# Weight loads ordered behind SyncE's rows, r.(u k) of two units on TensorE, and new tables for a planned RWKV-6 and FFN kernel

## The chip, the cores and the metric

The kernel runs on one core of one Trainium2 chip. The metric is the device time in microseconds (us) of an execution; for the kernel before it is 173.24 us, the median of 3 runs (173.14, 173.24, 174.6).

## What is computed

The reference has two stages. The first is a linear attention with a decaying state (RWKV-6), for 4 batches, 8 heads, 768 steps and head size 48:

```
for t in range(S):
    cur = u * k_t (outer) v_t
    y_t = r_t @ (state + cur)
    state = w_t[:, None] * state + k_t (outer) v_t
```

The second is a feed-forward network on the 3072 rows of y (384 wide; d_ff is 1024):

```
h = ((y @ w1) * (y @ w2)) @ w3
out = h @ w_out
```

All inputs are float32 in HBM, and the output is float32 of 3072 x 384.

## The kernel before, in words

**Units and chunks.** The 768 steps are cut into 6 chunks of 128. A unit is one chunk of one or two batches: units 0 and 1 are chunk 0 of batches 0 and 1, unit 2 is chunk 0 of batches 2 and 3, and units 3 to 12 are the two halves of the chunks 1 to 5. For each unit the function `unit` makes: `ln` (ScalarE: logarithm of w, line 638), `cs` and `ct` (TensorE: prefix sums of it with the triangular matrix LT, lines 647 and 654), `ne` and `e` (ScalarE: exponentials, 661 and 667), `Kt` (VectorE: k times the inverse decay, 672), transposes of r and Kt (`trr`, `trk`, 736 and 755) with their evictions `RT` and `KT` (741, 760), the product `m` of the two (774), its causal mask (`msk`: VectorE with the mask, line 780, or a copy on ScalarE, 783, with a select `maff` on GpSimd, 786), and `y` (809 for the state's part, 818 for the chunk's own). The state goes on by `kv` (864), `T` (871) and `S` (875).

**r.(u k).** The term with u is a number for each row and head, the sum over the head of r k u. The kernel makes it with `rk` (the product r k, line 677), `ruk` (times u_bc, which is u on all 128 partitions, 712) and `dg` (VectorE's sum over 48 elements, 716). `dv` multiplies v by it (718), and `yb` (830) adds dv to y. For the units in the set `PE_DIAG`, which is empty, the code has another way: transpose `rk` on TensorE (`rkt`), evict it (`rke`), multiply it by `u_blk`, a 384 x 8 block form of u (`d`), and copy the result out (`dcp`).

**Blocks.** y is transposed (`yt`, 847; `xT`, 852) and goes into 8 blocks of 128, 128, 256 and then 512 rows: units 0, 1, 2, then two units each. For each block the function `block` makes groups of `a` and `b` (x times w1 and w2, line 907), copies a out (`asb`, 916, two buffers), multiplies (`abT`, 920), and makes the output tiles `o` (929), `osb` (937) and their stores (942). Instead of two products, w3 and w_out are multiplied once: for each of 8 slices of w3, `wt` transposes it (596), `w3Te` evicts, `wm` multiplies it with w_out (608) and `w34e` evicts (613). No `o` can start before all 8 slices of w34 are there. The group a or b number z of a block needs one half of w1 or w2 (`w1_0`, `w1_1`, `w2_0`, `w2_1`).

**Loads.** The rows of w, k, r and v are loaded per unit for chunk 0 (`win_0` to `vin_2`), and by whole chunks afterwards (`win_3` is chunk 1, `win_5` chunk 2, and so on). Only `win_0` and `win_1` are issued by SyncE (`SP_LOADS`); all others, w1 and w2 in two halves, w3 in four quarters (`w3_0` to `w3_3`, each for two slices), w_out (`wo`) and u go out on GpSimd's queue, between GpSimd's own arithmetic. The rows of chunk 3 lie in the memory of w3 and wait for all `wt`.

**Order.** The order of all work is not written by hand. Each step is an `op` with an engine, an assumed duration, what it reads and writes, and a priority: its place in the program plus `RANK` of its kind plus `STEP` of its name; the smaller goes first. `Program.schedule` (from line 241) plays the steps in assumed time: on each engine that is free it takes the ready step of least priority whose PSUM banks can be had. GpSimd issues no load while the assumed end of its queue lies over `AHEAD` = 6000 ns ahead. `late` adds a dependency to the planner that the data don't have. The order found is then emitted; on the chip each engine works through its own list in order and waits for data. For loads the base of the priority is -10000 plus the place in `LOADS`. `ENGINE` says for the steps that can run on two engines which one takes them.

Of the kernel before, what the change touches and what calls it, by code (L numbers as in the profile page):

```python
# [16 lines left out]
    "KT": -38550, "Kt": -111832, "RT": 5515, "S": -11396, "Sb": 6495, "Sc": -932, "T": -60474, "a": -27703,  # L17
    "abT": -127179, "asb": -32208, "b": -15810, "cs": -59092, "ct": -970, "dg": 88898, "dtk": 10929, "dtr": -20063,
    "dty": -16475, "dv": -5126, "e": -21254, "gate": -14530, "kv": -15949, "ln": 72613, "m": -36962, "maff": -125562,
    "mask": 13249, "msk": -38101, "ne": -7835, "o": 62061, "ones": 17890, "osb": -54919, "pads": -19246, "rk": 73060,  # L20
    "rpad": 11555, "rpads": 6817, "ruk": 32687, "state": -53300, "store": 4513, "table": 12635, "trk": -56488,
    "trr": -71123, "ub": -15816, "ubc": 5038, "w34e": -43757, "w3Te": -48083, "wm": 54280, "wt": -87740,
    "xT": -131752, "y": -73194, "yb": -115233, "ys": 35037, "yt": -99587,
# [3 lines left out]
    "table": 70008.5, "ones": 60179, "LT": -1.5, "I128": 4.5, "pads": 98002, "rpads": 71930, "state0": 136111,  # L27
    "mask": 73935.5, "u": -1, "ub": 82542, "ubc": 76980.5, "w1_0": -1, "w1_1": -5, "wo": -2, "w3_0": -22, "w3_1": -3,
    "gate": 32463, "wt_0": 154172.5, "w3Te_0": 129818, "wm_0": 15188, "w34e_0": 129029, "wt_1": 154703,
    "w3Te_1": 130597.5, "wm_1": 15215.5, "w34e_1": 147138, "wt_2": 157233, "w3Te_2": 152054, "wm_2": 14976.5,  # L30
    "w34e_2": 148425.5, "wt_3": 157108, "w3Te_3": 153375, "wm_3": 15191, "w34e_3": 146990.5, "wt_4": 157683.5,
    "w3Te_4": 133999, "wm_4": 15136, "w34e_4": 145249, "wt_5": 157815.5, "w3Te_5": 149717, "wm_5": 15123.5,
    "w34e_5": 148851, "wt_6": 158569, "w3Te_6": 133971.5, "wm_6": 16223.5, "w34e_6": 144357.5, "wt_7": 158300,
    "w3Te_7": 149762, "wm_7": 14896, "w34e_7": 144603, "rpad3": 93022.5, "win_0": 21, "kin_0": 1, "rin_0": -0.5,
    "vin_0": -1, "ln_0": 2548, "cs_0": 125775.5, "ct_0": 66598, "ne_0": 83308.5, "e_0": 103240.5, "Kt_0": 194792.5,
    "rk_0": 10112.5, "ruk_0": 50257, "dg_0": -1654, "dv_0": 81249.5, "trr_0": 137833.5, "RT_0": 77645,
    "trk_0": 123546.5, "KT_0": 120493.5, "m_0_0": 103205.5, "msk_0_0": 121058, "maff_0_0": 201058.5, "y_0": 139438,
    "yb_0": 202437, "yt_0": 164599.5, "xT_0": 214714, "kv_0": 82166, "T_0": 143490.5, "S_0": 86842, "Sc_0": 83411.5,
    "a_0_0": 92637, "b_0_0": 83851, "asb_0_0": 114728.5, "abT_0_0": 214609, "a_0_1": 94836, "b_0_1": 80692,
    "asb_0_1": 115024.5, "abT_0_1": 209346, "o_0_0": 10003.5, "osb_0_0": 157512, "store_0_0": 4916, "win_1": 17,  # L40
    "vin_1": 5, "ln_1": 3415.5, "cs_1": 126255, "ct_1": 67602, "ne_1": 83529, "e_1": 104051, "Kt_1": 194830.5,
    "rk_1": 14562.5, "ruk_1": 47917, "dg_1": -5616, "dv_1": 92256.5, "trr_1": 137223.5, "RT_1": 81684,
    "trk_1": 124248, "KT_1": 120444, "m_1_0": 105234, "msk_1_0": 120873, "maff_1_0": 201454, "y_1": 141265.5,
    "yb_1": 203525, "yt_1": 164161, "xT_1": 214216.5, "kv_1": 84030.5, "T_1": 148735.5, "S_1": 86860.5,
    "Sc_1": 83039, "a_1_0": 97109, "b_1_0": 83800.5, "asb_1_0": 113342.5, "abT_1_0": 215398.5, "a_1_1": 91588,
    "b_1_1": 85615, "asb_1_1": 113497, "abT_1_1": 201257, "o_1_0": 9463, "osb_1_0": 159063.5, "store_1_0": 1566.5,
    "win_2": -4, "kin_2": -1, "rin_2": -7, "vin_2": 3, "ln_2": 10032, "cs_2": 125219.5, "ct_2": 68023.5,
    "ne_2": 90468.5, "e_2": 103110, "Kt_2": 192412.5, "rk_2": 3076, "ruk_2": 55529, "dg_2": -8338.5, "dv_2": 92032.5,
    "trr_2": 138240.5, "RT_2": 82374.5, "trk_2": 122481.5, "KT_2": 121357, "m_2_0": 102992, "msk_2_0": 124482,
    "maff_2_0": 212398, "m_2_1": 101072.5, "msk_2_1": 121512.5, "maff_2_1": 200856, "y_2": 143006.5, "yb_2": 197826,  # L50
    "yt_2": 168808.5, "xT_2": 219125.5, "kv_2": 83980, "T_2": 147552, "S_2": 98226.5, "Sc_2": 81915.5,
    "a_2_0": 97125.5, "b_2_0": 85352.5, "asb_2_0": 114484.5, "abT_2_0": 209778, "a_2_1": 91099, "b_2_1": 79819,
    "asb_2_1": 114887.5, "abT_2_1": 209146.5, "a_2_2": 97517, "b_2_2": 85273, "asb_2_2": 113263, "abT_2_2": 232260,
    "a_2_3": 97213.5, "b_2_3": 84677, "asb_2_3": 113260.5, "abT_2_3": 201082.5, "o_2_0": 8844.5, "osb_2_0": 158890.5,
    "store_2_0": 1560.5, "o_2_1": 9477.5, "osb_2_1": 156818.5, "store_2_1": 1516, "win_3": -6, "kin_3": -1,
    "rin_3": -1, "vin_3": 3, "ln_3": 10067, "cs_3": 123222, "ct_3": 70704.5, "ne_3": 90160, "e_3": 103517,
    "Kt_3": 199901.5, "rk_3": 8960.5, "ruk_3": 45468, "dg_3": -15223, "dv_3": 79040.5, "trr_3": 140863,
    "RT_3": 68568.5, "trk_3": 126558.5, "KT_3": 112504.5, "m_3_0": 106283, "msk_3_0": 141483, "maff_3_0": 211595.5,
    "m_3_1": 106688, "msk_3_1": 143460.5, "maff_3_1": 203735, "ys_3": 34763.5, "y_3": 142623, "yb_3": 200956,
    "yt_3": 168610.5, "xT_3": 217450.5, "kv_3": 85570, "T_3": 146670.5, "S_3": 89980, "Sc_3": 86574, "ln_4": 9654.5,  # L60
    "cs_4": 128220.5, "ct_4": 70214.5, "ne_4": 89951.5, "e_4": 103121.5, "Kt_4": 199813.5, "rk_4": 5913.5,
    "ruk_4": 49888, "dg_4": -15188, "dv_4": 110729.5, "trr_4": 140354, "RT_4": 68490, "trk_4": 125796,
    "KT_4": 143661.5, "m_4_0": 106275, "msk_4_0": 142101.5, "maff_4_0": 211692.5, "m_4_1": 106372.5,
    "msk_4_1": 141939.5, "maff_4_1": 211792, "ys_4": 34948.5, "y_4": 143017.5, "yb_4": 200903.5, "yt_4": 169292,
    "xT_4": 216637, "kv_4": 85986.5, "T_4": 134260, "S_4": 94111, "Sc_4": 102131.5, "a_3_0": 97359.5,
    "b_3_0": 86039.5, "asb_3_0": 133262, "abT_3_0": 231821.5, "a_3_1": 98771.5, "b_3_1": 86942, "asb_3_1": 136083,
    "abT_3_1": 229014.5, "a_3_2": 99107, "b_3_2": 86889, "asb_3_2": 134171.5, "abT_3_2": 229364, "a_3_3": 98952,
    "b_3_3": 87455, "asb_3_3": 134988.5, "abT_3_3": 229202.5, "o_3_0": 9791, "osb_3_0": 157499.5,
    "store_3_0": 4960.5, "o_3_1": 9352.5, "osb_3_1": 157275, "store_3_1": 4700, "o_3_2": 9888.5, "osb_3_2": 156319.5,
    "store_3_2": 4817, "o_3_3": 11928, "osb_3_3": 157320.5, "store_3_3": 5242.5, "win_5": 91976.5, "kin_5": 95199,  # L70
    "rin_5": 87329.5, "vin_5": 96011.5, "ln_5": 31462, "cs_5": 129257.5, "ct_5": 72093, "ne_5": 111671,
    "e_5": 124931.5, "Kt_5": 216926, "rk_5": 32516, "ruk_5": 56279.5, "dg_5": 14395, "dv_5": 109999, "trr_5": 142134,
    "RT_5": 96247, "trk_5": 127883, "KT_5": 140462.5, "m_5_0": 108808.5, "msk_5_0": 141236.5, "maff_5_0": 225164,
    "m_5_1": 108320, "msk_5_1": 140542.5, "maff_5_1": 224679.5, "ys_5": 38812, "y_5": 144993.5, "yb_5": 219879.5,
    "yt_5": 170492.5, "xT_5": 234218, "kv_5": 87022, "T_5": 162591, "S_5": 99705.5, "Sc_5": 103063.5, "ln_6": 29771,
    "cs_6": 129221.5, "ct_6": 71742.5, "ne_6": 111649.5, "e_6": 124630, "Kt_6": 216456, "rk_6": 15353.5,
    "ruk_6": 72232, "dg_6": 16055.5, "dv_6": 94137.5, "trr_6": 142019, "RT_6": 99915, "trk_6": 127371.5,
    "KT_6": 142440, "m_6_0": 108259.5, "msk_6_0": 140086.5, "maff_6_0": 225008, "m_6_1": 107960, "msk_6_1": 140043,
    "maff_6_1": 223327, "ys_6": 36889.5, "y_6": 144567.5, "yb_6": 219458, "yt_6": 171191.5, "xT_6": 235962.5,
    "kv_6": 86830.5, "T_6": 162909.5, "S_6": 99533, "Sc_6": 103343.5, "a_4_0": 98375.5, "b_4_0": 89760.5,  # L80
# [79 lines left out]
DMA_KR = set(range(9, 13))  # L160
DMA_Y = set(range(9, 13))
DMA_R = set(range(9, 13))
PE_DIAG = set()

BLOCKS = [[0], [1], [2], [3, 4], [5, 6], [7, 8], [9, 10], [11, 12]]

# [189 lines left out]
def kernel(  # L356
# [13 lines left out]
    nc = tc.nc  # L370
# [601 lines left out]
    with tc.manual_schedule():  # L972
        for o in order:
            o.fn(o.eng) if o.alt else o.fn()
# [30 lines left out]
```

## Time and profile before

| | |
|---|---|
| median of the runs | 173.24 us |
| the profiled execution | 174.64 us |
| its span, first to last instruction | 172.9 us |
| TensorE busy | 154.2 us (89%), 1696 matmuls |
| VectorE busy | 123.1 us (71%) |
| ScalarE busy | 99.2 us (57%) |
| GpSimd busy | 106.7 us (62%) |
| mean granted TensorE clock | 0.98 |
| GpSimd's DMA queue | 79024 packets, 15.86 MB |

In the profile PE is TensorE's matmul, PEld its weight load, DVE VectorE, ACT ScalarE, POOL GpSimd and SP SyncE; "POOL L549 kin" is the issue of a load, not its transfer. Times count from the start of the span. In the rows by stage the numbers are: stage, its length, then busy us (and instructions) of PE, PEld, DVE, ACT and POOL, the granted TensorE clock, the DMA share and GB/s. In a timeline a row is start, duration, engine, line, operation, output and inputs, shapes and count. The chain of waits is the work that ended last, followed back from the end: start, duration, what.

### The profile page before, as it was taken

The numbers are of one execution on the slowest core, as the hardware profiler recorded it, in microseconds if no ns is written. First come the engines' busy times: TensorE is split into PE (matmuls) and PEld (weight loads), VectorE is DVE, ScalarE is ACT, GpSimd is POOL, SyncE is SP. The second block draws the span as 40 slices with busy tenths as digits, with TensorE's granted clock in tenths as the row PEclk, the third lists the DMA queues.
The fourth block names the chain that finished last, engine by engine and source line by source line (L and its number), as shares of the span: only waits on it lengthen the run. The fifth ranks groups of instructions, "written<-read, shape, count | busy, mean of one in ns | idle before, by whom it ended". The sixth has DMA issues, their size and how long they took to land.

```text
span 172.9 us, 4084 instructions
## 1 busy us (share of the span) xinstructions
PE 154.2 (89%) x1696; PEld 98.8 (57%) x1708; DVE 123.1 (71%) x155; ACT 99.2 (57%) x134; POOL 106.7 (62%) x90
## 2 busy tenths in 40 slices
PE   0466489999989999999999999999999999999991
PEld 0254368998667666646675555645556455455560
DVE  5076995979897289999777997896689574544310
ACT  4437776674616977569669656957457524232331
POOL 7999985769796999599879969724413600000000
PEclk9999957999999999999999999999999999999999
DMA  6999999999999999999999998698135802111132
GB/s 93 154 190 189 227 179 169 160 207 172 203 182 178 102 144 127 211 185 216 171 186 249 133 89 46 127 187 198 38 64 101 238 20 48 25 49 45 45 122 107
DMA packets 96363, 24.12 MB, mean 139 GB/s; under 512 B 88632, under 2 KB 94264, under 8 KB 96344
## 3 DMA queue, kind: packets, MB, share of 16 engines
q0 software_dynamic: 79024, 15.86, 110.6%
q1 hardware_dynamic: 17320, 8.00, 18.9%
q8 instruction: 13, 0.21, 0.5%
q14 instruction: 6, 0.05, 0.1%
HBM read 27.79 MB, written 4.72 MB: 188 GB/s over the span
## 4 chain that ended last, share of the span: by engine, by line
PE 60%; DMA 12%; DVE 11%; POOL 10%; issue 4%; ACT 1%; DVEq 0%; POOLq 0%; ACTq 0%
PE banks L907 29%; PE banks L929 11%; PE banks L608 6%; DMA w_bf<-in_v_dram 6%; DMA kin<-in_k_dram 4%; PE banks L818 2%; POOL rin L549 2%; DVE Mbf L780 2%; POOL Mbf L786 2%; DVE abT L920 2%; DMA KRT<-Kt 2%; PE banks L774 2%; PE banks L596 2%; PE banks L654 2%; PE banks L864 2%
## 5 line engine op out<-in xcount | busy, mean ns | idle before, releaser
L907 PE MATMUL banks<-xT,w_bf 128*128 128x512 bf16 (+2 forms) x372 | 68.1, 330 | 1.0 <-DVE abT L920 0.2
L907 PEld LDWEIGHTS <-w_bf 128*128 128x128 bf16 x384 | 33.9, 101 | 26.4 <-issue 1.3
L920 DVE TENSOR_TENSOR abT<-a_sb,banks 128x1024 bf16<-128x1024 f32 (+1 forms) x28 | 29.8, 1067 | 21.0 <-PE banks L907 18.9
L916 ACT COPY a_sb<-banks 128x1024 f32<-128x1024 f32 (+1 forms) x28 | 24.8, 891 | 25.1 <-PE banks L907 21.4
L929 PE MATMUL banks<-w,abT 128*128 128x384 bf16 x192 | 34.0, 326 | 0.0
L929 PEld LDWEIGHTS <-abT 128*128 128x128 bf16 x192 | 18.3, 98 | 11.8
L786 POOL TENSOR_SCALAR_AFFINE_SELECT Mbf<-Mbf 128x1024 bf16<-128x1024 bf16 x14 | 15.3, 1099 | 7.8 <-ACT Mbf L783 7.8
L937 ACT COPY osb<-banks 128x384 f32<-128x384 f32 x20 | 9.6, 480 | 16.4 <-PE banks L929 16.4
L783 ACT CAST Mbf<-banks 128x1024 bf16<-128x1024 f32 x14 | 13.9, 1018 | 2.1 <-PE banks L774 2.0
L718 POOL TENSOR_TENSOR dv<-vin,dg 128x768 bf16<-128x768 bf16 (+1 forms) x7 | 10.0, 1431 | 6.6 <-DMA xT<-dv 3.4
L667 ACT ACTIVATE eT<-banks 128x1024 f32<-128x1024 f32 (+1 forms) x13 | 12.4, 956 | 2.4 <-PE banks L654 2.4
L654 PE MATMUL banks<-LT,lw 128*128 128x128 bf16 x96 | 8.0, 227 | 6.4 <-ACT lw L638 6.4
L780 DVE TENSOR_TENSOR Mbf<-banks,mask 128x1024 bf16<-128x1024 f32 x10 | 12.0, 1218 | 1.3 <-PE banks L774 1.3
L661 ACT ACTIVATE banks<-banks 128x768 f32<-128x768 f32 (+1 forms) x13 | 9.7, 749 | 4.9 <-PE banks L647 4.8
L830 DVE TENSOR_TENSOR dv<-banks,dv 128x768 bf16<-128x768 f32 (+1 forms) x13 | 11.6, 890 | 1.2 <-PE banks L818 1.1
L716 DVE TENSOR_REDUCE dg<-rk 128x16 f32<-128x768 bf16 (+1 forms) x13 | 11.5, 887 | 0.3
L638 ACT ACTIVATE lw<-win 128x768 bf16<-128x768 f32 (+1 forms) x11 | 8.3, 787 | 5.6 <-DMA win<-in_w_dram 5.6
L608 PE MATMUL banks<-wo_bf,w3T 128*128 128x384 bf16 x64 | 11.2, 326 | 0.0
L677 POOL TENSOR_TENSOR rk<-rin,kin 128x768 bf16<-128x768 bf16 x6 | 9.9, 1649 | 1.8 <-DMA rin<-in_r_dram 1.8
L601 ACT COPY w3T<-banks 128x1024 bf16<-128x1024 bf16 x7 | 6.9, 1014 | 7.1 <-PE banks L596 7.1
L654 PEld LDWEIGHTS <-lw 128*128 128x128 bf16 x96 | 6.3, 102 | 7.8 <-ACT lw L638 6.9
L672 DVE TENSOR_TENSOR Kt<-kin,banks 128x768 bf16<-128x768 bf16 (+1 forms) x11 | 9.5, 875 | 1.5 <-DMA kin<-in_k_dram 1.4
(83 smaller groups left out, 241.5 us busy)
## 6 DMA issues: line engine op xcount, KB each, us to landing
out_dram<-osb SPq DMA_DIRECT2D x24, 192.0 KB, 2.1
win<-in_w_dram POOLq DMA_DIRECT2D x4, 768.0 KB, 9.6
w_bf<-in_moe_w_dram POOLq DMA_DIRECT2D x4, 512.0 KB, 9.6
w_bf<-in_moe_w_dram POOLq DMA_DIRECT2D x4, 384.0 KB, 9.1
kin<-in_k_dram POOLq DMA_DIRECT2D x4, 384.0 KB, 7.7
rin<-in_r_dram POOLq DMA_DIRECT2D x4, 384.0 KB, 8.5
vin<-in_v_dram POOLq DMA_DIRECT2D x4, 384.0 KB, 8.7
wo_bf<-in_moe_w_out_dram POOLq DMA_DIRECT2D x1, 768.0 KB, 10.5
```

The source lines that it names most:

```text
L608: nc.tensor.matmul(o[:, :DM], lhsT=w3T[fi % 2][:, gi, :], rhs=wo_bf[:, gi, :], start=(gi == 0), stop=(gi == FI - 1))
L654: nc.tensor.matmul(o[:, b, q, :], lhsT=LW[:, b * H + 2 * q:b * H + 2 * q + 2, :].rearrange("t h d -> t (h d)"), rhs=LT, start=True, stop=True)
L667: nc.scalar.activation(ET[:, :, 1:], o[:, :nb * HP, :], Act.Exp)
L716: op("DVE", dve(N), lambda: nc.vector.reduce_sum(dgs, rks, axis=AX.X), r=[f"rk{s}"], w=[f"dg{s}"], prio=pr + 9, name=f"dg_{t}")
L780: nc.vector.tensor_mul(Mbf[m].rearrange("s j q t -> s (j q t)"), o.rearrange("s j f -> s (j f)"), mask.rearrange("s q t -> s (q t)"))
L783: nc.scalar.copy(Mbf[m].rearrange("s j q t -> s j (q t)"), banks[:, g.at(MM):g.at(MM) + 2, :])
L786: nc.gpsimd.affine_select(Mbf[m].rearrange("s j q t -> s (j q) t"), Mbf[m].rearrange("s j q t -> s (j q) t"), compare_op=Alu.is_gt, fill=0 ...
L830: nc.vector.tensor_add(ybs.rearrange("t b (q e d) -> t e (b q) d", e=2, d=D), o, dvs.rearrange("t (b q e) d -> t e (b q) d", b=nb, e=2))
L907: nc.tensor.matmul(o[:, q * T // TB, q % (TB // T), :], lhsT=wt[:, di, fi * P:(fi + 1) * P], rhs=xT[x][:, di, :T], start=(di == 0), stop=( ...
L916: nc.scalar.copy(a_sb[sa][:, :nbk * TB], banks[:, g.at(A):g.at(A) + nbk, :].rearrange("p k t -> p (k t)"))
L920: nc.vector.tensor_mul(abT[x][:, f[0]:f[0] + G, :T].rearrange("p i t -> p (i t)"), a_sb[sa][:, :nbk * TB], banks[:, g.at(Bk):g.at(Bk) + nb ...
L929: nc.tensor.matmul(banks[:, g.at(O), :DM], lhsT=abT[x][:, fi, tt * P:(tt + 1) * P], rhs=w34[:, fi, :], start=(fi == 0), stop=(fi == FI - 1))
```

## The change

Four things are done together. First, `wload` (w1, w2, w_out, w3) and the loads of w on GpSimd's queue get `late=SP_ROWS`: in the planner they become ready only when SyncE's two loads of w have ended. Second, `PE_DIAG` becomes {1, 2}: units 1 and 2 form r.(u k) by TensorE. Third, `RANK`, `STEP` and `ENGINE` are replaced throughout. Fourth, code for filler matmuls in TensorE's idle places comes in (`idle`, `fill`, a tile `warm`), with `WARM` and `FILL` both 0.0.

```diff
 STEP = {
-    "mask": 73935.5, "u": -1, "ub": 82542, "ubc": 76980.5, "w1_0": -1, "w1_1": -5, "wo": -2, "w3_0": -22, "w3_1": -3,
...
+    "mask": 57278, "u": 6, "ub": 71274, "ubc": 93101, "ublk": 75393.5, "ublk2": 108242.5, "w1_0": -2, "w2_0": 2,
+    "w1_1": -12.5, "w2_1": -2, "wo": -1, "w3_0": -4, "w3_1": -2, "w3_2": -1, "w3_3": -1, "gate": 22348.5,
...
+    "abT_1_1": 217906.5, "o_1_0": -4539, "osb_1_0": 161989, "store_1_0": 1175.5, "win_2": -3, "kin_2": 2,
+    "rin_2": -11, "vin_2": 3, "ln_2": -13119, "cs_2": 124194, "ct_2": 65213, "ne_2": 81535.5, "e_2": 111671,
...
 ENGINE = {
-    "ruk_0": "DVE", "dv_0": "POOL", "KT_0": "ACT", "msk_0_0": "DVE", "xT_0": "ACT", "S_0": "POOL", "osb_0_0": "ACT",
-    "rk_1": "DVE", "ruk_1": "DVE", "dv_1": "DVE", "KT_1": "ACT", "msk_1_0": "ACT", "xT_1": "ACT", "S_1": "DVE",
-    "osb_1_0": "ACT", "rk_2": "POOL", "ruk_2": "DVE", "dv_2": "POOL", "KT_2": "ACT", "msk_2_0": "DVE",
...
+    "ruk_0": "DVE", "dv_0": "DVE", "KT_0": "ACT", "msk_0_0": "ACT", "xT_0": "ACT", "S_0": "DVE", "osb_0_0": "ACT",
+    "rk_1": "DVE", "rke_1": "ACT", "dcp_1": "ACT", "dv_1": "DVE", "KT_1": "DVE", "msk_1_0": "ACT", "xT_1": "DVE",
+    "S_1": "POOL", "osb_1_0": "ACT", "rk_2": "DVE", "rke_2": "DVE", "dcp_2": "ACT", "dv_2": "DVE", "KT_2": "ACT",
...
-PE_DIAG = set()
+PE_DIAG = {1, 2}
+
+WARM, FILL = 0.0, 0.0
...
+    SP_ROWS = [f"SP{x}_{t}" for x, t in sorted(SP_LOADS)]
...
         op(eng, 60 if eng == "SP" else 650 + 270 * nb, lambda: e.dma_start(dst[:, b0 * H:(b0 + nb) * H, :D], ap),
-           r=FREED if c % NI == NI - 1 else (), w=[f"{src}in{c % NI}_{b}" for b in range(b0, b0 + nb)] + ["rows_" + src] * (c == NC - 1), prio=turn_of(f"{src}in_{t}"),
+           late=SP_ROWS if src == "w" and eng == "POOL" else (),
+           r=FREED if c % NI == NI - 1 else (), w=[f"{src}in{c % NI}_{b}" for b in range(b0, b0 + nb)] + ["rows_" + src] * (c == NC - 1) + [f"SP{src}_{t}"] * (eng == "SP"), prio=turn_of(f"{src}in_{t}"),
...
-        op("POOL", 800, lambda: nc.gpsimd.dma_start(dst, src), w=[key], prio=turn_of(key), dma=nbytes / 381.0, lag=1200.0, name=key)
+        op("POOL", 800, lambda: nc.gpsimd.dma_start(dst, src), late=SP_ROWS, w=[key], prio=turn_of(key), dma=nbytes / 381.0, lag=1200.0, name=key)
...
+    gaps = g.idle(order, FILL)
     with tc.manual_schedule():
+        if gaps:
+            nc.vector.memset(warm, 1.0)
         for o in order:
+            if o in gaps:
+                fill(*gaps[o])
             o.fn(o.eng) if o.alt else o.fn()
```

The new function `idle` walks TensorE's part of the order and stops at the first step for which the time is over its argument:

```
found, t = {}, self.FIRST["PE"]
for o in order:
    if o.eng != "PE":
        continue
    if t > until:
        break
```

`FIRST["PE"]` is 900.0. The entries of `STEP` that the order of the loads follows from, those that are not in the lines above (an entry that isn't in a table counts as 0):

| | before | after |
|---|---|---|
| kin_0, rin_0, vin_0 | 1, -0.5, -1 | none, -2, 5 |
| win_1, kin_1, rin_1, vin_1 | 17, none, none, 5 | 17, -4, -3, 2 |
| win_2, kin_2, rin_2, vin_2 | -4, -1, -7, 3 | -3, 2, -11, 3 |
| win_3, kin_3, rin_3, vin_3 | -6, -1, -1, 3 | -4, -1, none, 5 |
| win_0, LT, I128 | 21, -1.5, 4.5 | 7, 0.5, 1.5 |

## The prediction

> **What bounds the kernel now.** I read the busy table by stage first, because the page's averages mix a start in which TensorE waits with a long part in which it doesn't.
>
> ```profile
> 0.00:14.60 14.60, 6.03 (x54) 4.35 (x54) 6.32 (x24) 6.36 (x10) 13.39 (x20) 1.00 1.54 145
> 14.60:21.40 6.80, 3.23 (x50) 2.50 (x50) 6.59 (x9) 4.84 (x8) 6.80 (x8) 0.98 1.28 226
> 21.40:28.20 6.80, 5.98 (x67) 5.00 (x68) 6.36 (x9) 4.24 (x7) 4.71 (x4) 0.52 1.75 182
> 28.20:57.60 29.40, 28.66 (x446) 23.64 (x443) 24.10 (x32) 17.34 (x27) 23.30 (x20) 1.00 1.83 176
> 57.60:169.50 111.90, 110.26 (x1085) 63.36 (x1094) 79.75 (x83) 65.97 (x85) 58.45 (x42) 1.00 1.13 122
> ```
>
> The columns are PE, PEld, DVE, ACT, POOL, then granted clock and DMA. From 28.2 to 169.5 us PE is busy 138.92 of 141.3 us: there only PE's amount of work counts. Before 28.2 it is busy 15.24 us, 5.98 of them at half clock. So time can be won in two ways: PE's steady work starts earlier, or work moves into its idle start. In 14.6 to 21.4 DVE is busy 6.59 of 6.80 us, and POOL all of it.
>
> The chain of waits says what holds the start:
>
> ```profile
> 1.32 0.89 POOL w_bf L555
> ...
> 8.00 6.75 DMA kin<-in_k_dram
> 14.76 0.02 issue
> 14.78 0.07 DVE Kt L672
> 14.84 0.41 issue
> 15.25 1.22 DVE Mbf L780
> 16.47 0.60 DVE KRT L741
> 17.07 2.14 DVE rk L677
> ```
>
> POOL's first load (the w3 quarter) stands in front of everything; kin of unit 1, issued at 8.00, lands at 14.76; then DVE carries the chain, with one multiply at 2.14 us. The timelines of DVE and POOL show why that multiply is slow:
>
> ```profile
> 16.98 2.21 DVE L677 TENSOR_TENSOR rk<-rin,kin 128x384 bf16<-128x384 bf16 x1
> 17.30 1.67 POOL L677 TENSOR_TENSOR rk<-rin,kin 128x768 bf16<-128x768 bf16 x1
> ```
>
> The DVE form takes 0.35 us in its other occurrence (10.37); here it ends only when POOL's multiply of unit 2 has ended. Last, PE at the start of its steady work:
>
> ```profile
> 23.54 1.46 PE L907 MATMUL banks<-xT,w_bf 128*128 128x128 bf16 x12
> 26.52 1.49 PE L907 MATMUL banks<-xT,w_bf 128*128 128x128 bf16 x12
> 28.68 0.83 PE L907 MATMUL banks<-xT,w_bf 128*128 128x128 bf16 x12
> ```
>
> Adding each issue to its time to landing in the DMA view gives landings: w3_0 8.5, kin_0 9.3, rin_0 10.0, vin_0 10.7, rin_2 12.2, win_2 14.05, kin_1 14.8, rin_1 15.4, kin_2 16.6, w1_1 18.2, win_3 21.5, w1_0 23.2, vin_1 23.9, w2_0 25.9, vin_2 27.2, w2_1 29.1, kin_3 32.2, rin_3 35.5, wo 39.3, w3_1 41.8, vin_3 44.6, w3_2 47.1, w3_3 49.5. Block 0's first products start 0.3 us after w1_0 and its next group 0.6 us after w2_0: the queue of loads sets them.
>
> **What the Trainium skill says.** "SBUF — State Buffer", Who interferes with whom: VectorE with two SBUF inputs and a GpSimd instruction that reads SBUF exclude each other for the whole instruction. The pair above agrees (2.21 against 0.35 us). "TensorE: Matmul & The Clock Gate", Part 1: the clock starts at half and is released by about 3.4 us of activity. The trace agrees in kind: twelve 128-column matmuls take 1.46 us at clock 0.52 and 0.83 at 1.00. "DMA: Bandwidth & Descriptors", Queues, rings and completion order: descriptors are consumed in ring order. The landings above follow the order of issue.
>
> **Part 1, the loads.** `late=SP_ROWS` adds a dependency for the planner, and so an order; by the code no data joins the two, so I expect no wait on the chip. SyncE's two loads finish in the planner near 4.7 us, so POOL serves other rows till then. Sorting base + STEP of the new tables by hand, with that gate, gives rin_2, kin_0, rin_0, kin_1, w1_1, LT, rin_1, I128, win_2, u, vin_0, vin_1, w1_0, kin_2, win_3, w2_1, vin_2, w2_0, kin_3, w3_0, wo, rin_3, w3_1, w3_2, w3_3, vin_3. I re-add the landings with each load's own increment in the old list (w3 quarter 2.5, as w3_1 behind wo; w1/w2 halves 1.6 to 1.95; a unit's rows 0.6 to 0.7, of two batches 1.2 to 1.5; win_2 1.85; win_3 3.3; kin_3 3.1; rin_3 3.3; wo 3.8), starting at 8.5 - 2.5 = 6.0: kin_0 8.1, kin_1 9.5 (was 14.8), w1_1 11.1, vin_0 14.5 (was 10.7), vin_1 15.2 (was 23.9), w1_0 16.9 (was 23.2), kin_2 18.1 (was 16.6), vin_2 24.7 (was 27.2), the last w2 half 26.6 (was 29.1); then kin_3 29.7, w3_0 32.2, wo 36.0, rin_3 39.3 (was 35.5), w3_3 46.8, vin_3 49.9 (was 44.6). All of w1 and w2 is there 2.5 us earlier: **-2.5 us**, if PE can use it. LT goes behind five issues (1.2+0.9+0.9+0.9+0.8 us from 1.32, so about 6.3 instead of 2.6) and the first matmuls with it from 4.3 to about 6.4; that is hidden, since kin_0 lands only at 8.1.
>
> The price: w3_0 had let PE do eight plus eight transposes (L596) at 11.16 and 12.84, in idle time. They move into the steady part, 1.00 us for 16 in the chain: **+1.0**.
>
> **Part 2, r.(u k) of units 1 and 2.** DVE loses two multiplies (0.36, 0.55) and two reductions (0.55, 0.95): 2.41 us. It gains u_blk's copy and rke_2, which the trace doesn't show; by the copy row 128x768 (0.55) and the planner's 0.18, 0.7. Unit 2's first multiply comes to DVE (0.55) and takes the collision of 2.21 - 0.35 = 1.86 us with it. Net on DVE -3.0 us within a stretch where it is full. ACT gains rke_1 (0.48) and two tiny copies; it has 2 us free there. POOL gains two small selects (0.36 each by L477), loses 1.67. PE gets the values of units 1 and 2 earlier, but also needs weights, so I count half: **-1.5** (0 if the weights come last anyway, -3.0 if DVE is all). PE gains 9 transposes at 0.056 and 9 matmuls of 8 columns; nearest row L818, 16 in 0.40, 0.025 each: 0.7 us, more than half of it before PE is full: **+0.3** (0 to 0.7). A d-chain is rk, transpose, evict, product, copy, against the old multiply and reduction: longer for one unit[...], but behind it waits only dv, which needs vin (15.2, 24.7).
>
> **Part 3, orders and engines.** M of unit 0 goes to ACT plus a select on POOL, and POOL's queue then holds vin_1, w1_0, kin_2, win_3, w2_1, vin_2 in front of it: about 16.4, so M is ready at 17.5, y_0 at 17.7, xT_0 at about 19.3 (was 22.6). PE's products can start there, with both w1 halves in; two a-buffers and the missing w2 let it run only a_0_0, a_0_1, then b_0_1, a_1_1, b_1_1 until 26.6. POOL in all does fewer tensor operations (one rk, one ruk, three S less, one dv more; about -4 us of 107), DVE six more evictions of L937 (0.556 against 0.480): both are off the path while PE is full. The last eviction goes to DVE: **+0.1**. Rows of units 3 and 4 come 4 to 5 us later, behind w3_0 and wo; in 26.6 to 36.0 PE has the rest of blocks 0 to 2 (7.3 us), K transposes, prefix sums and two w3 transposes (3.5), so 10.8 us of work for 9.4 us: **+0.2**, up to +4. Clock: PE ran half-clocked from 21.4 to 28.2, and a new density may end this sooner or later: **0** (-2 to +2). `FILL` = 0 ends `idle` at its first step, so the filler does nothing.
>
> **Sum.** -2.5 + 1.0 - 1.5 + 0.3 + 0.2 + 0.1 + 0 = -2.4 us. The profiled execution took 174.64 us with a span of 172.9; it would become 172.2 and 170.5. The runs' median is 173.24, 1.4 less than the profiled time, so the forecast is 173.24 - 2.4 = **170.8 us**. With 1% being about what a measurement of this kernel can tell from no change, that means under 171.5 is faster and over 175.0 slower.
>
> **The rivals.** A, hidden anyway: POOL's select of unit 0 (behind six issues) and the u row (now tenth) hold y_0 and dv_0, so that xT_0 stays near 22.6, and the two w3 transposes are paid. For it: POOL is 6.80 of 6.80 busy there. Against: POOL's issues are short enough to be done by 16.4. Then -2.5 is lost and +1.0 stays, with part of DVE's gain: 173.5. B, larger gain: PE starts at 19.3, the clock is released before the full part and all DVE's gain counts: -2.5 + 1.0 - 3.0 - 2.0 = -6.5, so 166.7; I give 167.3. C, slower: PE runs dry between blocks 0 to 2 and units 3 and 4, since rin_3 and vin_3 are now behind w3_0, wo and the other quarters. The cover is 10.8 - 9.4 = 1.4 us; each us that wo or rin_3 lands later beyond that is lost. From 2.4 + 1.4 = 3.8 us on it decides against the change; at 6.6 us late the time is 173.24 + 2.8 = 176. For it: the queue already takes 8 to 12 us from issue to landing, and POOL issues between its own arithmetic. Against: wo landed at 39.3 before and was first used at 42.5, so PE had slack to it.
>
> **How the numbers follow.** Forecast 0.50 (its own range 168.8 to 172.3), B 0.15, A 0.17, C 0.18. Leaving out the far ends of B and C gives 167.2 to 175.3. Faster: B and four fifths of the forecast, 0.15 + 0.40 = 0.55; same: the last fifth, 0.10, and 0.15 of A = 0.25; slower: C and the rest of A, 0.18 + 0.02 = 0.20.
>
> **What would show it.** kin_1 landing near 9.5 and w2 complete near 26.6 in the DMA view; no DVE multiply of 2.2 us before 28; the first L907 near 19.3 to 20; rows L596 all after 30; L608 starting near 36 to 38. Wrong: a first L907 later than 22, or PE less than 9 tenths busy between 28 and 42 (C), or the half clock reaching past 28.

## The result and the profile after

The changed kernel takes 179.29 us (median of 4 runs, 178.45 to 180.41), the kernel before in the same session 173.92; the ratio is 1.031, 95% interval 1.022 to 1.040. It is slower by 5.4 us where 170.8 was forecast. Medians and ratios of all runs below leave out the slow executions, those more than 1.5% above the fastest of their kernel. The profiled execution took 179.71 us with a span of 178.0. The lines of the kernel after are 28 higher than before around the units and blocks: L935 are block products (L907 before), L957 the output products (L929), L965 their evictions (L937), L970 their stores, L764 the transposes of r (L736), L866 SyncE's DMA transposes of the values (L838).

The busy table by stage of the kernel after, with the columns of the one shown before (PE, PEld, DVE, ACT, POOL, clock, DMA share, GB/s):

```profile
0.00:14.60 14.60, 6.40 (x65) 4.45 (x65) 6.86 (x26) 7.38 (x12) 13.41 (x20) 1.00 1.60 151
14.60:21.40 6.80, 5.12 (x61) 4.67 (x58) 5.32 (x12) 3.71 (x8) 6.72 (x8) 1.00 1.43 208
21.40:28.20 6.80, 6.09 (x120) 5.26 (x119) 5.37 (x8) 6.59 (x11) 4.07 (x5) 1.00 2.12 169
28.20:57.60 29.40, 29.30 (x414) 23.26 (x413) 23.25 (x33) 17.70 (x26) 22.64 (x18) 1.00 1.85 185
...
84.50:95.30 10.80, 7.96 (x101) 6.87 (x101) 4.19 (x7) 5.67 (x8) 6.57 (x4) 0.68 1.95 209
...
125.50:154.00 28.50, 25.51 (x278) 14.22 (x281) 19.86 (x18) 12.45 (x15) 5.82 (x5) 1.00 0.31 74
```

Two of these stages of the kernel before, in the same table:

```profile
84.50:95.30 10.80, 10.75 (x135) 7.08 (x135) 8.48 (x11) 7.55 (x12) 9.06 (x7) 1.00 1.96 214
...
125.50:154.00 28.50, 27.95 (x261) 15.06 (x263) 19.77 (x18) 12.24 (x16) 5.16 (x4) 1.00 0.33 76
```

The start is better than it was: up to 28.2 us PE is busy 17.61 us instead of 15.24, and from about 21.6 on at full clock. (The clock column reads 1.00 ahead of that too, but it doesn't count the half speed in which PE begins: eight matmuls of 128 columns take 1.06 us at 18.28 below, and 0.61 at 83.87.) The time is lost in two later stages, in which the kernel before had PE busy nearly without a break: 84.5 to 95.3, where PE loses 2.8 us of busy time and the rest runs at a mean clock of 0.68, and 125.5 to 154, where it loses 2.4 us.

PE's own timeline shows where (start, duration, line, operation, count; in brackets the idle time ahead of it and what ended that):

```profile
18.28 1.06 PE L764 MATMUL banks<-I,rin 128*128 128x128 bf16 x8
...
21.23 1.00 PE L935 MATMUL banks<-xT,w_bf 128*128 128x128 bf16 x12
...
83.87 0.61 PE L682 MATMUL banks<-LT,lw 128*128 128x128 bf16 x8
87.34 1.01 PE L764 MATMUL banks<-I,w_bf 128*128 128x128 bf16 x8 [2.86 <-ACT osb L965]
...
93.17 1.53 PE L957 MATMUL banks<-w,abT 128*128 128x384 bf16 x8
...
134.00 2.75 PE L935 MATMUL banks<-xT,w_bf 128*128 128x512 bf16 x12 [1.65 <-DMA xT<-dv]
...
153.65 2.53 PE L935 MATMUL banks<-xT,w_bf 128*128 128x512 bf16 x11 [1.18 <-DMA xT<-dv]
```

Three stalls: A of 2.86 us, B of 1.65, C of 1.18. The kernel before has no wait over 0.71 us on PE after 28 us. ScalarE's timeline of the kernel after, at stall A:

```profile
86.81 0.86 ACT L965 COPY osb<-banks 128x384 f32<-128x384 f32 x2 [3.24 <-DMA out_dram<-osb]
```

The chain of waits through stall A and stall B, from the kernel after (start, duration, what):

```profile
78.30 0.47 DVE osb L965
...
78.79 8.00 DMA out_dram<-osb
...
86.81 0.49 ACT osb L965
...
87.34 1.01 PE banks L764 x8
...
127.65 1.19 SPq L866
...
130.23 1.19 SPq L866
...
131.48 2.39 DMA xT<-dv
```

**Stall A.** Four SBUF buffers take the output tiles in turn, and each tile's buffer is its number in the program modulo 4 (`so = tiles_out[0] % 4`). The new order runs block 2's tile 0 late, so the tiles are evicted into buffers 0, 1, 3, 2, 1, 2, 0, 3. Tile o_2_0 (buffer 2) is evicted at 78.30; its store is issued at 78.79 and lands 8.00 us later, and o_3_2, the next but one on its way out, wants buffer 2 again. ScalarE, which is to evict it, stands 3.2 us for that store, and behind it everything in its queue; PE stands because its next PSUM bank is not free. "DMA: Bandwidth & Descriptors", Queues, rings and completion order, in the Trainium skill says that each DMA engine goes round the queues that have work, packet by packet. The trace agrees only in that stores are slower beside loads: the median store took 2.1 us before and 3.0 after, and this one, issued beside GpSimd's row loads, 8.00. But from 78.9 to 81.5 us, with the store issued, 3200 packets of GpSimd's queue moved and none of SyncE's; what held the store for so long is not shown. From 86.5 to 93.3 the clock is half: L764 takes 1.01 us for eight matmuls, where eight of L682 took 0.61 before the gap.

**Stalls B and C.** The values of the last units go through SyncE's DMA transposes, four in a row for two units, which stand in SyncE's queue for about 1.2 us each, one behind the other. The planner counts 400 ns for one. It placed block 6's first products (a_6_1, a_6_0) ahead of block 5's output tiles; on the chip the transposed values are later than it believes, and PE stands. The order before had block 5's four output tiles there, which need nothing of these values:

```profile
129.06 1.46 PE L929 MATMUL banks<-w,abT 128*128 128x384 bf16 x8
...
130.81 4.06 PE L929 MATMUL banks<-w,abT 128*128 128x384 bf16 x24
```

### The profile page after: what moved, and what is told of

Same layout as the page of the kernel before. It is cut to its first block, busy times and chain, and to the rows that moved or that the text cites. A ratio compares the mean times of both kernels' runs of the same rounds, so it can differ in the third digit from the quotient of the medians.

```text
span 178.0 us, 4121 instructions
## 1 busy us (share of the span) xinstructions
PE 157.1 (88%) x1714; PEld 101.7 (57%) x1726; DVE 124.7 (70%) x165; ACT 95.5 (54%) x129; POOL 103.1 (58%) x87
## 4 chain that ended last, share of the span: by engine, by line
PE 50%; POOL 18%; DVE 10%; DMA 7%; issue 7%; SPq 4%; ACT 3%; POOLq 0%; DVEq 0%
PE banks L935 23%; PE banks L957 12%; DMA out_dram<-osb 4%; SPq L866 4%; POOL kin L576 4%; DVE abT L948 3%; DMA xT<-dv 3%; POOL win L576 2%; PE banks L846 2%; POOL vin L576 2%; POOL rin L576 2%; PE banks L764 2%; POOL Mbf L814 2%; PE banks L783 2%; PE banks L802 2%
## 5 line engine op out<-in xcount | busy, mean ns | idle before, releaser
L935 PE MATMUL banks<-xT,w_bf 128*128 128x512 bf16 (+2 forms) x372 | 67.7, 325 | 3.8 <-DMA xT<-dv 2.8
L935 PEld LDWEIGHTS <-w_bf 128*128 128x128 bf16 x384 | 32.5, 98 | 28.3 <-issue 3.7
L948 DVE TENSOR_TENSOR abT<-a_sb,banks 128x1024 bf16<-128x1024 f32 (+1 forms) x28 | 29.7, 1065 | 12.1 <-PE banks L935 11.0
L957 PE MATMUL banks<-w,abT 128*128 128x384 bf16 x192 | 34.1, 327 | 0.0
L957 PEld LDWEIGHTS <-abT 128*128 128x128 bf16 x192 | 18.4, 98 | 12.5
L808 DVE TENSOR_TENSOR Mbf<-banks,mask 128x1024 bf16<-128x1024 f32 x11 | 13.3, 1220 | 5.6 <-PE banks L802 5.0
L746 POOL TENSOR_TENSOR dv<-vin,dg 128x768 bf16<-128x768 bf16 x7 | 10.4, 1491 | 8.1 <-DMA xT<-dv 5.0
L965 ACT COPY osb<-banks 128x384 f32<-128x384 f32 x14 | 6.6, 480 | 14.0 <-PE banks L957 10.0
L675 PE MATMUL banks<-lw,LT 128*128 128x384 bf16 x24 | 6.5, 356 | 7.1 <-POOL LT L499 6.5
L576 POOL DMA_DIRECT2D kin<-in_k_dram x7 | 9.8, 1405 | 2.2 <-issue 2.2
L576 POOL DMA_DIRECT2D rin<-in_r_dram x7 | 10.0, 1431 | 1.9 <-DMA vin<-in_v_dram 1.1
L705 POOL TENSOR_TENSOR rk<-rin,kin 128x768 bf16<-128x768 bf16 x5 | 8.7, 1760 | 3.6 <-DMA rin<-in_r_dram 3.6
L576 POOL DMA_DIRECT2D vin<-in_v_dram x7 | 9.8, 1395 | 1.8 <-issue 1.8
L965 DVE COPY osb<-banks 128x384 f32<-128x384 f32 x10 | 5.5, 554 | 7.4 <-PE banks L957 7.3
```

Of the source, the lines that this page charges most:

```text
L576: op(eng, 60 if eng == "SP" else 650 + 270 * nb, lambda: e.dma_start(dst[:, b0 * H:(b0 + nb) * H, :D], ap), late=SP_ROWS if src == "w" and ...
L808: nc.vector.tensor_mul(Mbf[m].rearrange("s j q t -> s (j q t)"), o.rearrange("s j f -> s (j f)"), mask.rearrange("s q t -> s (q t)"))
L935: nc.tensor.matmul(o[:, q * T // TB, q % (TB // T), :], lhsT=wt[:, di, fi * P:(fi + 1) * P], rhs=xT[x][:, di, :T], start=(di == 0), stop=( ...
L948: nc.vector.tensor_mul(abT[x][:, f[0]:f[0] + G, :T].rearrange("p i t -> p (i t)"), a_sb[sa][:, :nbk * TB], banks[:, g.at(Bk):g.at(Bk) + nb ...
L957: nc.tensor.matmul(banks[:, g.at(O), :DM], lhsT=abT[x][:, fi, tt * P:(tt + 1) * P], rhs=w34[:, fi, :], start=(fi == 0), stop=(fi == FI - 1))
L965: (nc.scalar.copy if eng == "ACT" else nc.vector.tensor_copy)(osb[so], banks[:, g.at(O), :DM])
```

## The experiments

Theory S, formed from the trace: the start is better by something near the forecast, and three stalls that come of the new orders (a buffer, and a cost that the planner has too low) take 7 us back. The rival R: the new orders are slower in many places, and the stalls are only where it shows.

**e1, eight output buffers.** `osb = many(8, ...)`, and the eviction and the store take `tiles_out[0] % 8`; the planner still counts four, so every list is the same.

> The changed kernel with eight output buffers osb in place of four; the planner still counts four, so every engine's list is the same. Theory S (a store that the row loads hold up keeps an osb buffer, ScalarE waits 3.2 us for it, TensorE 2.9 us for ScalarE, and then runs 6.8 us at half clock, which costs some 3.1 us more): 179.3 - 2.9 - 3.1 = 173.3 us, no half clock after 80 us. Theory R (TensorE is ahead of the rows of chunk 3 there and would wait for the next thing anyway, such as vin of unit 7 landing near 94): 177 us or more, with a wait of TensorE of 2 us or more between 85 and 97. Theory T (the DMA transposes at the end are the loss): 179.3 - 0, no change.

Measured: 174.93 us, ratio to before 1.0043 [1.0021, 1.0066], so stall A with its clock is worth 2.7%, 4.6 us. The waits between 84 and 97 are gone, the half clock too; B (1.66) and C (1.19) stay.

**e9, four buffers handed out as they are used.** That e1 has more buffers doesn't say that there were too few.

```
 def oev(eng, O=O, mine=mine):
+    mine.append(used[0] % 4)
+    used[0] += 1
-    (...)(osb[so], banks[:, g.at(O), :DM])
+    (...)(osb[mine[0]], banks[:, g.at(O), :DM])
```

> The changed kernel with its four output buffers, but handed out in the order in which the output tiles are evicted, not in the order in which the program names them. Theory S (the stall at 84.5 comes of the hand-out: a late tile holds the buffer that an early one wants): the 3.2 us wait of ScalarE and the half clock behind it go, about 175.0, as with eight buffers. Rival N (the number of buffers is what is short, since a store under load takes 8 us): part of the wait stays, 176.5 to 178.

Measured: 174.8 us, 1.0038 [1.0019, 1.0057], the same as with eight. The number of buffers was enough; which tile got which was wrong for the new order. PE's timeline of e9 at the place of stall A:

```profile
84.20 0.61 PE L764 MATMUL banks<-I,w_bf 128*128 128x128 bf16 x8
...
87.47 1.46 PE L957 MATMUL banks<-w,abT 128*128 128x384 bf16 x8
```

The stretch from these first L764 to the next L957 takes 87.47 - 84.20 = 3.27 us here, and 93.17 - 87.34 = 5.83 in the kernel after: the half clock costs 2.56 us, nearly as much as the 2.86 us gap ahead of it. Together 5.4 us; e9's span is 5.6 shorter. That is the profiled execution, with a mean clock of 0.981; the other three of the kernel after have 0.988 to 0.990, so that they lost less by the clock.

**e2, the transposes at their measured cost.** In the planner `op("SP", 400, ...dma_start_transpose...)` becomes 1250 for the values and 1320 for r and k.

> The changed kernel, but the planner counts SyncE's DMA transposes at 1250 to 1320 ns, as the profile shows them, in place of 400; that changes the order from the first of them on (three output tiles of block 5 go in front of block 6's first products) and nothing earlier. Theory T: the two waits for xT (1.65 and 1.18 us) go, 179.3 - 2.8 = 176.5 us. Theory S: also 176.5, since the part at 84 to 93 us is untouched. Theory R: 178 to 179.3, the waits move to the products' other inputs.

Measured: 177.35 us, 1.019 [1.0138, 1.0243]: 2.1 us less than the kernel after. The planner now puts block 5's tiles ahead of a_6_0. PE's timeline of e2, at stall A and at the old stall B:

```profile
87.77 0.61 PE L764 MATMUL banks<-I,w_bf 128*128 128x128 bf16 x8 [2.28 <-ACT osb L965]
...
89.39 1.03 PE L783 MATMUL banks<-I,Kt 128*128 128x128 bf16 x8
...
132.63 3.42 PE L957 MATMUL banks<-w,abT 128*128 128x384 bf16 x20 [0.22 <-DVE abT L948]
```

The waits for the values are gone (0.22 and 0.41 us are left, on other things), stall A is not. After its 2.28 us gap the clock is still full at first (0.61) and half later, from 89.3 to 92.7.

**e3 and e13, both.** e3 is e1 with e2, e13 is e9 with e2.

> Both edits together. If S and T are each right and independent: 179.3 - 6.0 - 2.8 = 170.5 us, which is below the kernel before. If R holds for one of them: 174 to 177.

> The changed kernel with the four output buffers handed out in the order of the evictions, and with SyncE's transposes entered in the planner at 1250 and 1320 ns. Theory S (the three stalls are the whole loss; the number of buffers does not matter): as with eight buffers and the same costs, about 172.9. Rival (eight buffers were needed as well once the stalls of the transposes are gone): 174 or more.

Measured: e3 172.96, 0.9936 [0.9913, 0.9959]; e13 172.99, 0.9917 [0.9889, 0.9946]. Both are faster than the kernel before, e13 by 0.83% or 1.4 us, with the change's loads, tables and sum on TensorE kept; only the lists from the first DMA transposes on are planned anew. The account is -1.4 for the change itself, +4.7 for A (1.0038 to 1.031) and +2.1 for B and C (0.9917 to 1.0038). That this makes +5.4 is no check, since each term is the step from one ratio to the next. What does test it is each part with the other gone, within one session: A is worth 4.4 us with B and C gone (e2 to e3), and B and C are worth 2.0 with A gone (e1 to e3), so the parts add. The sum in e3's expectation, 170.5, was 2.5 us too low because it priced A at 6.0 and B and C at 2.8. Theory R falls: with the stalls out, no net loss is left.

**e5, eight buffers in the kernel before.**

> The kernel before with eight osb buffers. Its only wait for a store is 0.3 us, on VectorE, so theory S gives no change: 173.2 to 173.9 us. A gain of over 1.5 us would mean that the buffers hold up the kernel in a way that the waits don't show.

Measured: 173.65, 0.9978 [0.9952, 1.0004]: no difference that is resolved. The buffers were no limit in the old order. Its profile has another use: its start is the code of the kernel before, yet PE ran at clock 1.00 from 21.4 to 28.2, where the profiled execution of before had 0.52, and its span is 171.9 against 172.9. About 1 us of the lead that the profile after shows in the start is thus the clock. The row of this stage in e5:

```profile
21.40:28.20 6.80, 4.20 (x75) 3.56 (x76) 6.36 (x9) 5.11 (x9) 5.20 (x4) 1.00 1.76 184
```

This half clock is not the accident of one execution. Of 172 executions of the kernel before, measured beside these experiments, 101 have a mean clock of 0.968 to 0.980, with a median of 174.72 us, and 43 have 0.996 or more, with 173.68. By the profiles, 0.980 is a start with some 6.8 us of half clock (before, e17), 0.997 one without (e5). The new order without stall A has 0.996 or more in all its 76 executions (e1, e3, e9, e13). So a part of what the change is worth is the clock that its start keeps: against the executions of the kernel before that kept it too, in the same session, e13 stands at -0.6 us (172.99 against 173.58) and e3 at -0.7 (172.96 against 173.69), about half of what they gain over all.

**e8 and e19, r.(u k) on TensorE in the kernel before.** `PE_DIAG = {1, 2}`, with `STEP` entries for the new instructions fitted so that everything else keeps its place; in e8 five steps still moved, because unit 0's values come sooner past VectorE. e19 puts those back; **e18** makes that order without the sum. A sixth step moved in e8 and is not put back in e19: GpSimd issues the load of unit 2's values ahead of its multiply for unit 2. In the kernel before, the multiply comes first (17.30) and the load after it (18.88).

> The kernel before with only r.(u k) of units 1 and 2 summed by TensorE; every other instruction keeps its engine and its place. The prediction's step: DVE's 2.4 us out of a full stretch are worth -1.5, TensorE's work costs +0.3, so about 172.7. Rival H (the loads of w1 and w2 set the start of block 0 and of block 1, so what DVE does ahead of them is hidden): no change, 173.9, or up to +0.4 for TensorE's added work.

> The kernel with r.(u k) of units 1 and 2 summed by TensorE, and those five steps put back where the kernel before has them (one PSUM bank chosen anew). Theory P: 173.0 to 173.5. Rival Q: 174.0 to 174.4. If both this and the run of the order alone are near 173.2, either way of getting the values of unit 0 past VectorE's queue is enough.

> The kernel before with the order of that run and without its sum: on VectorE the addition of unit 0 ahead of unit 1's u multiply; on TensorE y_0's transpose ahead of unit 1's scores and block 0's first products ahead of unit 2's; on ScalarE their evictions likewise. Theory P (the sum on TensorE takes VectorE's work away, and that is the gain): little, 174.0 to 174.4 against 174.3. Rival Q (the order is the gain): 173.0 to 173.5.

Measured: e8 173.23, 0.994 [0.9918, 0.9962]; e19 173.27, 0.9923 [0.9885, 0.9961]; e18 176.21, 1.0077 [1.0045, 1.011]. So the order of the five steps is not the gain, it costs 1.3 us by itself; the gain is that of the sum together with the sixth step. VectorE's timeline of e19, and GpSimd's:

```profile
17.40 0.35 DVE L677 TENSOR_TENSOR rk<-rin,kin 128x384 bf16<-128x384 bf16 x1
18.51 0.95 DVE L672 TENSOR_TENSOR Kt<-kin,banks 128x768 bf16<-128x768 bf16 x1 [0.76 <-ACT banks L661]
...
19.85 1.21 DVE L741 TENSOR_TENSOR KRT<-banks,eT 128x1024 bf16<-128x1024 bf16 x1
```

```profile
18.03 1.19 POOL L549 DMA_DIRECT2D vin<-in_v_dram  x1 [0.19 <-issue]
19.23 1.66 POOL L677 TENSOR_TENSOR rk<-rin,kin 128x768 bf16<-128x768 bf16 x1
```

VectorE's last row, r and k of unit 2 for TensorE, stands at 21.30 in the kernel before: 1.45 us later. The multiply that took 2.21 us there takes 0.35, since GpSimd's comes after it here. L672 stands at 19.51 there, so 1.00 of the 1.45 us is won ahead of it, where the pair and one u multiply stood, and the rest behind it. The runs do not separate what the sum is worth from what the parted pair is worth.

**e11, the pair that exclude each other, alone.** `rk_2` on VectorE in the kernel before, nothing else.

> The kernel before with one instruction moved: r.k of unit 2 on VectorE instead of GpSimd, so that the pair that exclude each other is gone. The multiply of 2.21 us should read about 0.35 to 0.55. Theory D (VectorE carries the chain in the start): 1 to 1.8 us faster, 172.1 to 172.9. Rival H (the loads set the start): no change, 173.9.

Measured: 174.08, 0.9976 [0.9948, 1.0005]: nothing that is resolved. VectorE's timeline of e11, and the row of the kernel before that answers to its second:

```profile
17.99 0.35 DVE L677 TENSOR_TENSOR rk<-rin,kin 128x384 bf16<-128x384 bf16 x1
...
19.54 0.95 DVE L672 TENSOR_TENSOR Kt<-kin,banks 128x768 bf16<-128x768 bf16 x1 [0.81 <-ACT banks L661]
```

```profile
19.51 0.95 DVE L672 TENSOR_TENSOR Kt<-kin,banks 128x768 bf16<-128x768 bf16 x1
```

The multiply is 1.86 us shorter, and yet the next large step starts at 19.54 instead of 19.51, because it waits for ScalarE's decays of unit 2. But ScalarE was late in this execution for another reason: SyncE's second load of w came late, and L638 for unit 1 started at 9.05 instead of 6.77. (e5, with the old start and the same late load, 8.81, has this step at 19.51 too, and its multiply takes 1.45.) Besides, unit 2's multiply now takes 0.55 us on VectorE, at 20.87, and L741 starts at 21.80 instead of 21.30. So e11 shows that trading the collision for this multiply gains nothing that is resolved; that the collision by itself costs nothing is not shown.

**e12, e14 and e17, the loads.** In the kernel before, `w3_0` goes behind the other loads of the start and its sixteen transposes behind block 1; all lists are otherwise kept.

```
+    for names, ahead in ((("w3_0",), "kin_3"), (("wt_0", "w3Te_0", "wt_1", "w3Te_1"), "trr_4")):
+        for x in names:
+            order.remove(at[x])
+            order.insert(order.index(at[ahead]), at[x])
```

e14 also moves `vin_1` ahead of `w1_1`; e17 is e14 with `w3_0` behind `kin_3` and the transposes ahead of `trr_3`.

> The kernel before with the first quarter of w3 loaded just ahead of unit 3's k instead of first of all, and its sixteen transposes and two evictions moved behind block 1; everything else keeps its engine and its place. The prediction's step: all of w1 and w2 2.5 us earlier, +1.0 for the transposes: -1.5, about 172.4. Rival H2 (TensorE cannot use the weights earlier, because the values and VectorE's work set the start): about +1.0, 174.9. Either way kin of unit 1 should land near 12.3 instead of 14.8.

> The kernel before with the late w3 quarter as in the last such run, and the values of unit 1 loaded ahead of w1. In that run TensorE stood 2.93 us at 23.89 for just these values. Theory V (the values of unit 1 take over the wait from the weights, and with both early the gain of the prediction's step appears): -1.0 to -1.5, 172.8 to 173.2. Rival W (VectorE's work takes over the wait in its turn): 173.6 to 174.2.

> The kernel before with the first w3 quarter loaded behind unit 3's k (ahead of its r), the values of unit 1 ahead of w1, and the quarter's sixteen transposes moved to just ahead of unit 3's r; all else as before. Theory L (the earlier trials lost their gain to unit 3's k, which still stood behind the quarter): the 1.95 us wait at 34.70 goes, and the step gives -1.0 to -1.5, 172.8 to 173.3. Rival W (whatever comes next takes the wait over): -0.4 as before, 173.9.

Measured: e12 173.96, 0.999 [0.9963, 1.0018]; e14 173.8, 0.9975 [0.9951, 0.9999]; e17 174.56 (four runs), 1.001 [0.995, 1.0069]. PE's timelines show where the 2.5 us went, in e12:

```profile
20.12 0.84 PE L907 MATMUL banks<-xT,w_bf 128*128 128x128 bf16 x12
23.89 0.36 PE L818 MATMUL banks<-vin,Mbf 128*128 128x48 bf16 x8 [2.93 <-DMA vin<-in_v_dram]
```

and in e14:

```profile
34.70 1.07 PE L755 MATMUL banks<-I,Kt 128*128 128x128 bf16 x16 [1.95 <-DVE Kt L672]
```

Block 0 starts at 20.12 instead of 23.54, and then PE stands for the values of unit 1, which in that list are still behind w1; with those early, it stands for unit 3's k, behind the w3 quarter. In e17 neither of these waits is left, and its profiled execution has a span of 171.5 us, but its four runs spread from 173.2 to 175.15, so that a gain or a loss of under 1 us is open.

**e15 and e16, all of it in the old order.** The loads, the sum on TensorE and the buffers by use, in the kernel before; e15 with the loads of e14, e16 with those of e17. In e15 one of the moved transposes takes a PSUM bank in which block 2 still has a product, so that part of block 2's output is not computed.

> The kernel before with the w3 quarter late, the values of unit 1 early, r.(u k) of units 1 and 2 summed by TensorE, and the output buffers handed out in the order of the evictions. Theory A (the gains of the start add up): -1.0 of TensorE's sum, -1.0 of the loads, -0.4 of the buffers, about 171.8. Rival O (the parts overlap, because each shortens the same wait): no better than the best part alone, 173.0 to 173.3.

> The same loads, with r.(u k) of units 1 and 2 summed by TensorE and the output buffers handed out in the order of the evictions. Theory A (the gains add up): -1.0 of TensorE's sum, -1.2 of the loads, -0.4 of the buffers, about 171.7. Rival O (they shorten the same wait): 173.0 to 173.3, no better than the best alone.

Measured: e15 175.43, 1.0076 [1.0053, 1.0099], with PE standing 1.67 us for unit 3's k at 34.56 and 1.57 us for the eviction of a moved transpose at 40.06; e16 173.0 (four runs), 0.9945 [0.9891, 1.0]. Rival O fits: the parts do not add up; that they shorten the same wait is the likely reason and not shown. None is better than e13, the change with its stalls mended.

## Why the prediction was wrong, step by step

- **The bound.** "There only PE's amount of work counts" was read off 138.92 of 141.3 us. It describes the old order. That PE hardly waits there was the work of that order, and the change replaces it.
- **Part 1, the loads (-2.5, +1.0).** The landings came as worked out: kin_1 at 8.5 (9.5 forecast), w1_0 at 16.2 (16.9), the last w2 half at 26.8 (26.6), kin_3 at 29.5 (29.7). The condition "if PE can use it" is where the size was off: on the old order the loads were worth between -0.9 and +0.3 us (e12, e14), since the next datum in PE's list took the wait over (e17, with both such waits gone, leaves it open). The first L935 came at 21.23, not 19.3 to 20: y_0 (L846) was even earlier than forecast, 16.49 against 17.7, but PE worked through prefix sums and transposes at half speed until then. `late=SP_ROWS` indeed makes no wait: without it the planner gives the new kernel the same list on every engine.
- **Part 2, r.(u k) (-1.5, +0.3).** Right in sign, and in size partly by luck: -1.2 forecast, 0.9923 [0.9885, 0.9961] in e19, -1.3 us. The measured figure has the clock in it, which the prediction priced apart, at 0: 18 of the 21 executions of the kernel before in that session have a mean clock of 0.980 or less, and none of e19's nine. Among the executions that kept the clock, e8's 173.41 stands against 173.69 of the kernel before, which is not resolved. Of the -3.0 counted on VectorE, e19 shows 1.45 by L741; how it divides between the sum and the pair is open. "SBUF — State Buffer", Who interferes with whom, in the Trainium skill holds for the pair itself: 2.21 us beside GpSimd's multiply, 0.35 without it (e11, e19).
- **Part 3, orders and engines (+0.1, +0.2).** This is the step that failed: "both are off the path while PE is full". The orders were costed only where they changed an engine's amount of work or a load's time, and outside the start at next to nothing. Evictions were counted by duration (six of 0.556 against 0.480) and not by which buffer each takes and when its store lands. The measured terms are +4.7 us for one buffer that comes round two stores too early, about half of it through the clock in the profiled execution, and +2.1 us for first products placed ahead of values that come later than the planner's price says (block 6's ahead of block 5's tiles, and stall C behind them).
- **The clock (0, -2 to +2).** It was looked at in the start alone, where it did get better, by some 0.5 to 0.9 us of the change's worth (e3, e13). It was lost at 86.5. "TensorE: Matmul & The Clock Gate", Part 1, in the Trainium skill has the clock fall after an idle window of about 3.4 us; here it was half from 2.0 us into a gap of 2.86 us on and, in e2, from 1.5 us after the end of one of 2.28. The measured gaps decide: one shorter than that window was enough to lose the clock, for 6.8 us and for 3.4. The gaps of B and C, 1.65 and 1.18 us, lost none.
- **The rivals.** C had the right sign for another reason: PE was to run dry at 28 to 42 us. It was busy 29.30 of 29.40 us from 28.2 to 57.6. A (hidden anyway) describes the loads on the old order. Of B, the clock did hold through 21.6 to 28, but PE's products did not start at 19.3. No case had a stall that the new order makes late in the kernel, and so none came near 179.29 for the reason that held.
- **The sum.** With the three stalls mended, the change is worth -1.4 us [-1.9, -0.9] (e13) where -2.4 was worked out. About half of it is the clock of the start, a term put at 0. Part 2 and the loads share the rest, in parts that the runs do not settle.

## What to carry to other kernels

Where a change brings new orders with it, walk each order for resources that come round in turn: list which buffer each tile takes in the order of execution, and how long the store that frees it takes beside the loads running then. Compare the planner's price of each kind of instruction with its row in the trace; a price that is three times too low does no harm until an order relies on it. On a kernel whose PE is full, price a gap by the clock as well: here 2.86 us of waiting cost 5.4 in the profiled execution. And before a profile's lead in a sparse start is put down to a change, look at the clock of many executions: here one start came in two kinds, 1 us apart.

## What was not expected of the hardware

A store of 192 KB on SyncE's queue took 8.00 us from issue to landing while GpSimd's row loads ran, against a median of 2.1 us in the kernel before; in the first 2.6 us of them no packet of its queue moved. A DMA transpose held SyncE's queue for about 1.2 us, four in a row for a pair of units, so that the last of them landed 6.2 us after the first was issued (127.65 to 133.87). One start of the kernel, the same code up to 57 us, ran from 21.4 to 28.2 at clock 0.52 in one execution and at 1.00 in another, and the mean clocks of 172 executions show both kinds often. The half clock came in stretches of 6.8 us (before, after, e17) or 3.4 us (e2).
